# Two early output stores cut into pieces of unequal row counts, in an attention and mixture-of-adapters kernel

## The chip, the core and the metric

The kernel runs on one core of a Trainium2 chip. The metric is the device time of one execution in microseconds (us), as the median of several runs. The core has five engines that run side by side: TensorE (PE in the profile, its weight loads PEld), VectorE (DVE), ScalarE (ACT), GpSimd (POOL) and SyncE (SP). Memory is moved by 16 DMA engines that all queues share. A transfer that is issued by SP goes into SP's queue (q1), one issued by POOL into POOL's queue (q0). Each DMA engine adds one to a transfer's semaphore when its own part has landed, so that a transfer is complete at a count of 16.

## What is computed

Four batches of 6400 rows and 256 channels go through a cross-covariance attention, and the result goes through a mixture of eight low-rank adapters:

```
qn = q / (norm(q, axis=1) + 1e-06);  kn = k / (norm(k, axis=1) + 1e-06)
s = kn.transpose(0, 2, 1) @ qn / tau            # 256 x 256 per batch
a = softmax(s);  x = (v @ a).reshape(25600, 256)
logits = x @ w_gate                              # 8 experts, the best 2 are kept
w = softmax over the 2 kept logits
delta = sum over the 2 kept e of w[e] * ((x @ A[e]) @ B[e])
out = x + delta                                  # 25600 x 256, float32
```

All of q and k of a batch must have been read before its 256 x 256 matrix is known, and v is then multiplied by it. So 78 MB are read and 26 MB are written.

## The kernel before, in words

A batch's 6400 rows lie on 128 partitions, 50 rows of 256 channels on each. q and k are loaded in three parts of 17, 17 and 16 of these 50 (cast to bf16 on the way, L578), v in five parts of 10 (also L578). The output leaves in the same five parts per batch: the store of part i of batch b, written (b, i) here, takes 128 partitions of 10 x 256 float32, so each partition gives one run of 10,240 bytes, a **row** of the store in what follows. With 16 DMA engines each engine moves eight such rows per store. The last two parts of the last batch leave in three smaller stores each.

For each batch, PE accumulates k'q, k'k and q'q (`do_G`, L593 to L602), the norms and the softmax follow on DVE and ACT, and then every part of v is transposed (L788), gated (L812 to L879) and multiplied into the output tile `y` (`do_Y`, L915 and L920). ACT or DVE copy it from PSUM (`do_Ye`, helper lines L769 and L771), and the store follows (`do_store`, L928).

The order on each engine is written out ahead of time by a small planner (`make_plan` and `Plan.run`): it simulates the five engines and the DMA, and takes on each engine the step of lowest rank that is ready. Loads are issued by POOL in a fixed order, at most eight in flight, stores by SP. A planned store is one step on SP whatever its number of DMA instructions is, so the planner's order doesn't depend on how `do_store` issues it.

Some stores are held back on purpose. `HOLD` names for such a store a load, and `do_hold` (L645) puts a DMA of 32 bytes on SP's queue that reads the end of that load's tile. As SP issues in order, the stores behind it wait until that load has landed. SP's queue around the change is:

- 77.92 us: store (0, 2)
- 78.33 us: hold for k part 2 of batch 1
- 78.97 us: store (0, 1), and at 91.01 us store (0, 3)
- 166.65 us: hold for k part 1 of batch 3
- 167.21 us: store (0, 0), computed long before and held, and at 167.89 us store (1, 0)
- 182.74 us: hold for k part 2 of batch 3, and from 183.34 us on the rest of the stores

DMAs of SP and ACT take eight semaphores in turn; the DMA that gets a semaphore again waits for the one that had it before, eight places ahead.

Of the kernel before, what the change touches and what calls it, by code (L numbers as in the profile page):

```python
# [32 lines left out]
class Clock:  # L33


    WINDOW, FIRST, LOW, HIGH = 3.413, 0.31, 0.5, 0.8

# [3 lines left out]
    def at(self, t):  # L41
        w = max(0, int((t - self.FIRST) / self.WINDOW) + 1)
        while len(self.cold) <= w:
            share = self.busy[-1] / self.WINDOW
            self.cold.append(share < (self.HIGH if self.cold[-1] else self.LOW))
            self.busy.append(0.0)
        return w

    def took(self, t, us):

        end, w = t, self.at(t)
        while us > 1e-9:
            pace = 2.0 if self.cold[w] else 1.0
            step = min(us * pace, max(self.FIRST + w * self.WINDOW - end, 1e-6))
            self.busy[w] += step
# [5 lines left out]
    def idle(self, t):  # L61

        w = self.at(t)
        return t - self.FIRST - (w - 1) * self.WINDOW - self.busy[w] > self.SPARE

# [165 lines left out]
def make_plan(B, order, ahead):  # L231
# [150 lines left out]
    for b in range(B):  # L382
        for i in range(NP):
            x = pos["v", b, max(g for g, (i0, _) in enumerate(V) if i0 <= i)]
            parts = UNITS if b == B - 1 and i >= NP - FINE else ((0, PC),)
            for c, n in parts:
# [25 lines left out]

PARTS = {(0, 0): ((0, 2), (2, 15)), (0, 2): ((34, 8), (42, 8)), (3, 2): ((34, 8), (42, 8))}
FINE = 2
FIRST = 4
OFF = {(0, 0, 'k'), (0, 0, 'q'), (0, 1, 'q'), (0, 2, 'k'), (0, 2, 'q'), (0, 4, 'q'), (0, 5, 'q'),
        (0, 6, 'k'), (0, 6, 'q'), (0, 7, 'k'), (0, 8, 'q'), (1, 0, 'k'), (1, 0, 'q'), (1, 1, 'q'),
# [41 lines left out]
def kernel(  # L459
# [11 lines left out]
    nc = tc.nc  # L471

    B, N, C = q.shape
    P = 128
# [15 lines left out]
    out_v = out.rearrange("(b p c) d -> b p c d", b=B, p=P)  # L490
# [44 lines left out]
    held = {}  # L535
# [25 lines left out]
    def do_load(s, what, b, i, c, n):  # L561
        if what == "v":
            t, src, c0 = sb(s, "v", (b, i), [P, PC * max(n for _, n in V), C], BF16), v_v, c
        else:
            t = sb(s, "qk", (what, b, i), [P, max(n for _, n in QK), C], BF16)
            src, c0 = {"q": q_v, "k": k_v}[what], QK[i][0]
            if (b, c) == (0, 0):
                n = FIRST
                if "first" not in W:
# [6 lines left out]
        if (what, b, i) in (("q", 0, 0), ("k", 0, 0)):  # L576
            c, n = FIRST, c + n - FIRST
        nc.gpsimd.dma_start(t[:, c - c0:c - c0 + n, :], src[b, :, c:c + n, :])  # L578
# [346 lines left out]

    def do_store(s, b, i, c, n):
        lo = i * PC + c
        nc.sync.dma_start(out_v[b, :, lo:lo + n, :], held["y", (b, i), ""][:, c:c + n, :])  # L928


    do = dict(load=do_load, wts=do_wts, sq=do_sq, add=do_add, red=do_red, n2p=do_n2p, hold=do_hold, warm=do_warm, cast=do_cast, G=do_G, accs=do_accs, n2=do_n2, rsqrt=do_rsqrt, rq_ps=do_rq_ps, s=do_s,
              exp=do_exp, recip=do_recip, aT_ps=do_aT_ps, aT=do_aT, waA_ps=do_waA_ps, waA=do_waA,
              a=do_a, ZL=do_ZL, ZLe=do_ZLe, T=do_T, Te=do_Te, log=do_log, loge=do_loge, Z=do_Z, Ze=do_Ze, gzT=do_gzT,
              gzTe=do_gzTe, Y=do_Y, Ye=do_Ye, store=do_store)
    for name in ("m1", "eq1", "lm", "m2", "mask", "msum", "t", "th", "g2"):
        do[name] = gate_step(name)
# [50 lines left out]
```

## Time and profile before

| what | value |
|---|---|
| median of 4 runs | 254.39 us (254.31 to 254.58) |
| the profiled execution's own time | 254.36 us |
| its span from the first to the last instruction | 252.6 us |
| PE busy | 218.4 us (86% of the span) |
| DVE, ACT, POOL busy | 192.5, 151.5, 27.0 us |
| moved by DMA | 66.70 MB counted at the SBUF side, mean 264 GB/s |
| granted TensorE clock, mean | 0.980 |

A page of the profile has the busy time per engine, the span cut into 40 equal slices (a digit is the busy share in tenths, 9 is 90% or more), the DMA queues, the chain of work that ended last, the costliest groups of instructions, and the DMA issues with their median time from issue to landing. Other views of the same trace give the waits, the instructions in order of time, and tables by stretch of time. The trace also has, for each transfer, the times of the 16 counts on its semaphore and, for each DMA packet, its queue, start, duration and size; it doesn't have the number of the DMA engine that moved it.

### The profile page before, as it was taken

To read this page: it belongs to the slowest core of one execution; us is meant where nothing else is said; L and a number is where in the kernel's file an instruction comes from. 1 tells how busy PE (TensorE), PEld (TensorE's weight loads), DVE (VectorE), ACT (ScalarE), POOL (GpSimd) and SP (SyncE) were. 2 spreads that over 40 slices of the span, in tenths; PEclk is the share of its full clock that TensorE was granted. 3 is DMA by queue.
4 is the path that set the end of the run, shared out by engine and by line. 5 is a ranking of instruction groups with operands and counts; after the bars stand their busy time and mean duration, and the time that the engine had idled before them with its cause. 6 is when DMAs were issued, how large, how long until landed. Compare 5 with 4: busy or idle time off the path is not lost.

```text
span 252.6 us, 5852 instructions
## 1 busy us (share of the span) xinstructions
PE 218.4 (86%) x2357; PEld 194.1 (77%) x2357; DVE 192.5 (76%) x528; ACT 151.5 (60%) x269; POOL 27.0 (11%) x54
## 2 busy tenths in 40 slices
PE   0273997888999998899999999889999979999980
PEld 0151884676999997799899899779999768999970
DVE  0055587979988996988999987689898889888830
ACT  5354435555877545785677757452784846557770
POOL 7002110040002002000500100500000000000000
PEclk9998599999999999999999999999999999999997
DMA  8999999999999999999999999999999999999995
GB/s 251 213 219 209 214 219 214 214 219 215 215 215 223 308 305 294 246 215 221 210 214 218 220 214 218 215 208 324 309 254 335 337 317 319 342 400 428 419 410 227
DMA packets 11243, 66.70 MB, mean 264 GB/s; under 512 B 1360, under 2 KB 1744, under 8 KB 6608
## 3 DMA queue, kind: packets, MB, share of 16 engines
q0 software_dynamic: 6912, 38.80, 74.4%
q1 hardware_dynamic: 3968, 26.87, 26.1%
q10 hardware_dynamic: 336, 0.66, 0.8%
q8 instruction: 18, 0.29, 0.4%
q14 instruction: 9, 0.07, 0.1%
HBM read 78.91 MB, written 26.21 MB: 416 GB/s over the span
## 4 chain that ended last, share of the span: by engine, by line
PE 75%; DVE 10%; DMA 8%; ACT 2%; issue 2%; POOL 1%; DVEq 0%; POOLq 0%
PE Y_ps L915 17%; PE acc L593 16%; DMA qk<-in_k_dram 8%; PE Y_ps L920 8%; PE T_ps L788 7%; PE ZL_ps L812 6%; PE gzT_ps L902 5%; PE acc L597 5%; PE acc L602 4%; DVE a_bf L763 2%; PE Z_ps L879 1%; PE n2p_ps L636 1%; PE log_ps L826 1%; PE warm_ps L777 1%; DVE ssq L627 1%
## 5 line engine op out<-in xcount | busy, mean ns | idle before, releaser
L593 PE MATMUL acc<-qk 128*128 128x256 bf16 x400 | 70.3, 284 | 17.4 <-DMA qk<-in_k_dram 9.9
L915 PE MATMUL Y_ps<-a_bf,vT 128*128 128x256 bf16 x400 | 60.0, 272 | 0.2 <-DVE acc_sb L710 0.2
L621 DVE TENSOR_TENSOR ssq<-ssq,sq 128x1280 f32<-128x1280 f32 (+1 forms) x27 | 43.3, 1604 | 19.7 <-ACT sq L615 19.7
L769 ACT COPY y<-Y_ps 128x512 f32<-128x512 f32 x79 | 46.1, 585 | 17.0 <-PE Y_ps L920 13.9
L593 PEld LDWEIGHTS <-qk 128*128 128x128 bf16 x400 | 34.7, 102 | 20.6 <-DMA qk<-in_k_dram 10.8
L615 ACT ACTIVATE sq<-qk 128x1280 f32<-128x1280 bf16 (+1 forms) x27 | 36.9, 1367 | 18.9 <-DVE ssq L621 16.8
L915 PEld LDWEIGHTS <-vT 128*128 128x128 bf16 x400 | 39.0, 98 | 4.6 <-issue 0.3
L920 PE MATMUL Y_ps<-ball,gzT 128*128 128x256 bf16 x200 | 38.2, 273 | 0.0
L597 PE MATMUL acc<-qk 128*128 128x128 bf16 x242 | 34.9, 226 | 0.0
L769 ACT COPY vT<-T_ps 128x512 f32<-128x512 f32 (+1 forms) x44 | 21.2, 510 | 11.7 <-PE T_ps L788 11.3
L788 PE MATMUL T_ps<-ident,v 128*128 128x128 f32 x200 | 27.5, 274 | 0.6 <-DVE waA_sb L757 0.4
L597 PEld LDWEIGHTS <-qk 128*128 128x128 bf16 x242 | 24.7, 102 | 3.8
L890 DVE TENSOR_TENSOR gz<-zl,gateg 128x256 bf16<-128x256 f32 x70 | 26.3, 444 | 0.3
L578 POOL DMA_DIRECT2D v<-in_v_dram x20 | 11.4, 575 | 130.7 <-PE T_ps L788 88.6
L602 PE MATMUL acc<-qk 128*128 128x128 bf16 x168 | 23.9, 225 | 0.0
L788 PEld LDWEIGHTS T_ps<-ident,v 128*128 128x128 f32 x200 | 22.3, 141 | 1.6 <-DVE waA_sb L757 0.6
L902 PE MATMUL gzT_ps<-ident,gz 128*128 128x128 f32 x100 | 20.9, 281 | 2.6 <-DVE gateg L868 1.4
L920 PEld LDWEIGHTS <-gzT 128*128 128x128 bf16 x200 | 19.6, 98 | 2.3
L812 PE MATMUL ZL_ps<-waA_sb,vT 128*128 128x136 bf16 x280 | 19.5, 223 | 1.7 <-DVE waA_sb L757 1.5
L812 PEld LDWEIGHTS <-vT 128*128 128x128 bf16 x280 | 17.7, 98 | 2.4 <-issue 2.2
L771 DVE COPY gzT<-gzT_ps 128x256 f32<-128x256 f32 (+1 forms) x40 | 15.0, 379 | 4.7 <-PE gzT_ps L902 3.1
L771 DVE COPY y<-Y_ps 128x512 f32<-128x512 f32 x21 | 14.5, 700 | 4.1 <-PE Y_ps L920 4.1
(80 smaller groups left out, 268.9 us busy)
## 6 DMA issues: line engine op xcount, KB each, us to landing
out_dram<-y SPq DMA_DIRECT2D x18, 1280.0 KB, 17.5
v<-in_v_dram POOLq DMA_DIRECT2D x20, 640.0 KB, 19.0
qk<-in_q_dram POOLq DMA_DIRECT2D x7, 1088.0 KB, 21.4
qk<-in_k_dram POOLq DMA_DIRECT2D x7, 1088.0 KB, 27.4
qk<-in_q_dram POOLq DMA_DIRECT2D x4, 512.0 KB, 20.0
qk<-in_k_dram POOLq DMA_DIRECT2D x4, 512.0 KB, 23.2
qk<-in_q_dram POOLq DMA_DIRECT2D x2, 1024.0 KB, 19.2
qk<-in_k_dram POOLq DMA_DIRECT2D x2, 1024.0 KB, 23.5
```

What stands on the lines that cost most here:

```text
L593: nc.tensor.matmul(acc[ic][:, 0:256], kt[:, j, ic::CC], qt[:, j, :], start=c == 0, stop=False, skip_group_check=True)
L597: nc.tensor.matmul(acc[ic][:, 256:384], kt[:, j, ic::CC], kt[:, j, ic::CC], start=False, stop=False, skip_group_check=True)
L602: nc.tensor.matmul(acc[ic][:, 384:512], qt[:, j, ic * P:(ic + 1) * P], qt[:, j, ic * P:(ic + 1) * P], start=False, stop=c == NC - 1, skip_ ...
L615: nc.scalar.activation(out[:, 0:n, :], t[:, j:j + n, :], ACT.Square)
L621: nc.vector.tensor_tensor(out=t, in0=t, in1=held["sq", (w, b, g), ""][:, 0:n, :], op=OP.add)
L769: nc.scalar.copy(out, in_)
L771: nc.vector.tensor_copy(out, in_)
L788: nc.tensor.matmul(ps[:, j, :], vt[:, c + j, :].bitcast(FP32), W["ident32"], is_transpose=True, start=(j == 0), stop=(j == n - 1))
L812: nc.tensor.matmul(ps[:, j, :], vT_of(b, i, c + j)[:, :, ic], st[b]["waA"][:, ic, :], start=(j == 0 and ic == 0), stop=(j == n - 1 and ic ...
L902: nc.tensor.matmul(ps[:, j, :], pairs[:, j * P:(j + 1) * P], W["ident32"], is_transpose=True, start=(j == 0), stop=(j == n // 2 - 1))
L915: nc.tensor.matmul(ps[:, j, :], vT_of(b, i, c + j)[:, :, ic], st[b]["a"][:, ic, :], start=(j == 0 and ic == 0), stop=False, skip_group_che ...
L920: nc.tensor.matmul(ps[:, j, :], pair[:, :, j], W["B"], start=False, stop=(j == 1), skip_group_check=True)
```

## The change

Two stores are no longer issued as one DMA of 128 rows. Store (0, 2) is issued as three DMAs of 112, 8 and 8 rows, store (0, 0) as four DMAs of 96, 8, 13 and 11 rows. All other stores are as before, and the same bytes go to the same places. A DMA of 112 or 96 rows is dealt to 16 DMA engines, one of 8, 13 or 11 rows, as the change has it, to the first 8, 13 or 11 of them, one row each.

```diff
 FINE = 2
+SPLIT = {(0, 2): ((0, 112), (112, 8), (120, 8)), (0, 0): ((0, 96), (96, 8), (104, 13), (117, 11))}
 FIRST = 4
...
     def do_store(s, b, i, c, n):
         lo = i * PC + c
-        nc.sync.dma_start(out_v[b, :, lo:lo + n, :], held["y", (b, i), ""][:, c:c + n, :])
+        for p, rows in SPLIT.get((b, i), ((0, P),)):
+            nc.sync.dma_start(out_v[b, p:p + rows, lo:lo + n, :], held["y", (b, i), ""][p:p + rows, c:c + n, :])
```

The built program differs in these five added DMAs on SP and in which of the eight semaphores each later DMA of SP takes; the order of the instructions on every other engine is the same.

## The prediction

> **What bounds the kernel now.** I read the chain that ended last first, by line and then for its last 28 us. From 24.9 us on it runs on PE with short stretches of DVE and ACT; its only long DMA piece is the first k load. So between 25 and 246 us the loads are early enough. The end of the chain, followed by the SP queue in order of time:
>
> ```profile
> 244.94 0.44 PE Y_ps L915 x4
> 245.37 0.23 PE Y_ps L920 x2
> 245.63 0.58 ACT y L769
> ```
>
> ```profile
> 245.59 1.47 SPq L928 DMA_DIRECT2D out_dram<-y  x2
> ```
>
> The last product ends at 245.6 us, its copy at 246.2, and the last store is issued at 246.24. The span is 252.6. The remaining 6.4 us hold no computation, which the table by stretch of time shows (PE, PEld, DVE, ACT, POOL busy, clock, DMA share, GB/s):
>
> ```profile
> 246.00:248.00 2.00, 0.00 (x0) 0.00 (x0) 0.00 (x0) 0.21 (x1) 0.00 (x0) 1.00 1.01 400
> 248.00:250.00 2.00, 0.00 (x0) 0.00 (x0) 0.00 (x0) 0.00 (x0) 0.00 (x0) 0.81 0.73 294
> 250.00:252.60 2.60, 0.00 (x0) 0.00 (x0) 0.00 (x0) 0.00 (x0) 0.00 (x0) 0.50 0.14 54
> ```
>
> All 16 DMA engines work until 248 us, three quarters of their time is used until 250, and then 0.14: few engines are still at work while the others are done. The waits on SP's queue say that the end stands on these stores:
>
> ```profile
> SPq L982 <- DMA out_dram<-y: 4.3, 5, 1.2
> ```
>
> How far the engines lie apart is in the 16 counts on the semaphore of the last store (us, sorted):
>
> ```
> 248.74 248.81 248.82 248.92 249.00 249.28
> 250.09 250.51 250.52 250.53 250.70 250.83 250.94
> 251.58 251.74 251.83
> ```
>
> Six are early, seven in the middle, three late. The last count comes 0.72 us before the span ends, and nothing but that count is waited for. So the kernel ends with its latest DMA engine, and evening out the engines is worth at most 251.83 less the mean of the sixteen, 250.18, that is 1.65 us. Compute can't be overtaken: the early engines land 2.5 us after the issue, so they are bound by the issue at 246.24.
>
> **Does a shift at 80 or 170 us live to the end?** An engine's shift is lost only where that engine runs dry. The page's DMA row has 9 in all slices between the first and the last, and q0 and q1 together take 100.5% of 16 engines' time:
>
> ```profile
> DMA  8999999999999999999999999999999999999995
> ...
> q0 software_dynamic: 6912, 38.80, 74.4%
> q1 hardware_dynamic: 3968, 26.87, 26.1%
> ...
> q8 instruction: 18, 0.29, 0.4%
> ```
>
> The counts agree. Between the loads that land at 119 and at 149 us the sorted distances of the engines stay equal to about 0.1 us but for single steps, and the stores that land at 226, 230, 233, 236 and 240 us all have four early counts within 0.4 us and the last three 3.6 to 4.0 us behind the first. I take a shift as lasting, for the late engines at nothing lost; the early ones do run dry after about 240 us, as their distance shrinks to 3.1.
>
> **The change part by part.**
>
> - Price of a row: late full stores land 3.05 us apart on one engine (229.52, 232.58, 235.63 for the first count), eight rows each, 0.38 us a row; a row's packet lasts 385 ns alone and 398 beside a load. I take 0.385.
> - Rows per engine in the two stores, 8 + 8 = 16 before. After, as the change has them dealt: engines 0 to 7 get 7+1+1 and 6+1+1+1, 18 rows (+0.77 us); 8 to 10 get 7 and 8, 15 (-0.385); 11 and 12 get 14 (-0.77); 13 to 15 get 13 (-1.155).
> - Five more DMAs on SP, at 0.33 to 0.59 us of issue each by the rows of SP's queue. At 78 us two of them push the hold from 78.33 to about 79.3 and store (0, 1) from 78.97 to 79.9. Store (0, 2)'s rows start at 81.4 and land at 87.2 at the earliest, so q1 has work on each engine meanwhile: nothing. At 167 us three push store (1, 0) from 167.89 to about 169.4; the rows ahead of it land at 176.3 at the earliest: nothing. Without that cover it would be 1.5 us on q1 alone, while q0 kept the engines busy. The hold at 182.74 waits for its load and doesn't move.
> - Semaphores: later DMAs of SP wait for another DMA eight places ahead. The nearest new pair is the store issued at 185.9 us behind the 11-row piece, which lands near 178; each has 7 us or more. ACT and DVE copies that write the two `y` buffers again now wait for three and four semaphores in place of one; the waits view has no wait of ACT or DVE for a store at all, so it costs at most a few 20 ns semaphore instructions.
> - Small transfers: each adds a 4-byte packet (9 to 22 ns) per engine used, at most 0.1 us in all. Store after store in the end phase follows 6 ns behind the other's 4-byte packet on the same engine, so a transfer has no gap of its own while a queue is full. The Trainium skill, "DMA: Bandwidth & Descriptors", section "Anatomy of one DMA", speaks against the change: about 2.0 us fixed per DMA. Were that paid on the engines five times, the sum would be 264 us; the 6 ns row says that it is latency, and is hidden here.
>
> **Which engines are late** decides, and the trace has no engine numbers. What it tells: already in the first loads one engine trails (first big load: 15 counts within 0.67 us, the last at 1.16). Then 18 instruction blocks of 16 KB (q8) come, one every 10 us or so, 0.9 to 1.0 us each, and each sets one engine back by about 1.1. The first eight go to engines that were not late by a block from an earlier one, and the next ones to engines already late: at 164 us seven engines are still within 0.93, nine at 1.28 to 2.46. So the blocks go around about eight engines, 18 = 8 + 8 + 2, and the late three are those with a third block and the one that trailed from the start. An engine that trails by one block's worth before the first block is where I put the block before it; the late three are then neighbours in this round. I choose the numbering 15, 14, 13 for them: the last-served engine from the start is 15, and the round runs down. That is a choice, not a reading. Two other numberings stand below as rivals.
>
> On that choice the Trainium skill, same page, section "Latency and other measured facts", has a rule: engines 7 and 15 are usually slower than the rest. For 15 it fits; an engine 7 among the late three would give 255.1 us. No view here shows the numbers.
>
> **Sum.** The late three land at 251.83 - 1.155 = 250.67, and 8 to 12, from the middle, at 250.94 - 0.385 = 250.56 at the latest. But engines 0 to 7 are eight and only six are early, so two of the seven in the middle get 0.77 more. As the engines without blocks are the early ones, I take for them the two lowest of the middle, 250.09 and 250.51: 250.86 and 251.28. The last of these is then the new end, a gain of 251.83 - 251.28 = 0.55. The profiled execution took 254.36, the median is 254.39: **253.8 us**. The ends of this case are 253.2, where those two are so dry at the end that their shift is lost (only the late three count, 1.16 of gain), and 254.2, where a higher one of the middle is among them (250.94 + 0.77 = 251.71, 0.12 of gain).
>
> **Rivals.**
>
> 1. **A late engine has a number of 0 to 7.** It gets two rows more, 251.83 + 0.77: 255.1 us, slower. Any of the eight with a count over 251.06 is enough. For it: only three of sixteen are late, and by numbers alone they rarely all fall on 13 to 15. Against: seven engines get no block up to 164 us and the late three are neighbours, so all three lie among the engines with blocks.
> 2. **The round runs up**, late are 15, 8 and 9: the last two lose one row, 251.74 - 0.385 = 251.36, gain 0.47: 253.9.
> 3. **Rows of the 112- and 96-row DMAs cost more**, as engines take 7 or 6 neighbouring partitions in place of 8. No row shows it; below by nothing, above by the longest row or load packet of that stretch, 551 against 398 ns, 13 x 0.153 = 2.0 us on each engine: 251.83 - 1.155 + 2.0, 255.2 us. It decides from 89 ns a row.
> 4. **The pieces aren't dealt as said**: if an 8-, 8-, 8-, 13- and 11-row piece each went to one and the same engine, it would have 61 rows, 45 x 0.385 = 17 us more: some 265 to 271 us, less what later loads hide.
>
> **How the numbers follow.** The forecast's case 0.60 (0.44 of it faster by over 0.2%, which is 0.5 us and about what a measurement of this kernel can tell from no change; 0.16 within), rival 1 0.20 (slower), rival 2 0.10 (0.03 faster, 0.07 within), rival 3 0.07 and rival 4 0.03 (slower). Faster 0.47, same 0.23, slower 0.30. The range 253.2 to 255.2 takes in the forecast's own ends, rivals 1 and 2, and rival 3 up to its upper price.
>
> **What would show it.** Right: issue of the last store still at 246.2 us; its 16 counts span some 2.5 us instead of 3.1, the last near 251.3 and no group of three behind the rest; share of DMA after 250 us below 0.14. Wrong numbering: the last count at 252.5 or above with the first unchanged. Rival 3: the packets of the two split stores longer than 398 ns, and all 16 counts later. Wrong altogether: the last store issued at another time, or PE waiting for a load after 25 us.

## Result and profile after

The changed kernel takes 254.69 us (median of 41 runs, 254.38 to 255.61), the kernel before 254.48 us beside it (61 runs, 254.25 to 254.68). The ratio is 1.001, with a 95% interval of 1.0006 to 1.0015: slower by about 0.1%, which is within the 0.2% that the prediction took as no change. A gain of 0.55 us was forecast, and 0.2 us were lost. The ratios here and below compare fast runs with fast runs, and they can differ from the quotient of the two medians by 0.001, in the two slowest kernels by up to 0.002.

The profiled execution of the changed kernel took 254.86 us, 0.50 more than that of the kernel before and 0.17 above its own median, so it shows more than the typical loss. Its chain ends as before, one copy and a store, only later:

```profile
245.68 0.44 PE Y_ps L916 x4
246.12 0.23 PE Y_ps L921 x2
246.37 0.58 ACT y L770
```

SP's queue in order of time has the added DMAs in its counts (x3 and x5 where one and two stores stood), and, in a second window, the last two stores:

```profile
76.50 1.08 SPq L930 DMA_DIRECT2D out_dram<-y  x3
...
167.49 2.15 SPq L930 DMA_DIRECT2D out_dram<-y  x5
```

```profile
246.33 0.99 SPq L930 DMA_DIRECT2D out_dram<-y  x2
```

The last store is issued at 246.98 us (246.24 before). The table of the end by stretch of time, with the same columns as in the prediction:

```profile
246.00:248.00 2.00, 0.33 (x4) 0.05 (x1) 0.00 (x0) 0.89 (x2) 0.00 (x0) 1.00 1.05 420
248.00:250.00 2.00, 0.00 (x0) 0.00 (x0) 0.00 (x0) 0.00 (x0) 0.00 (x0) 0.60 0.85 337
250.00:253.10 3.10, 0.00 (x0) 0.00 (x0) 0.00 (x0) 0.00 (x0) 0.00 (x0) 0.50 0.12 46
```

The engines do lie closer together: more is moved from 248 to 250 us (337 GB/s, 294 before). But the stretch behind 250 us is 3.1 us long and not 2.6. The wait at the end and the load of the queues are as before:

```profile
SPq L984 <- DMA out_dram<-y: 4.6, 5, 1.2
```

```profile
DMA  8999999999999999999999999999999999999995
...
q0 software_dynamic: 6912, 38.80, 74.3%
q1 hardware_dynamic: 4016, 26.87, 26.1%
...
q8 instruction: 18, 0.29, 0.4%
```

q1 has 48 packets more, which are the small packets at the ends of the added DMAs; the bytes are the same. The mean row took 394.2 ns (393.4 before). The 16 counts on the last store's semaphore:

```
249.49 249.49 249.51 249.53 249.65 249.97 250.05 250.17
250.51 250.51 250.56 250.61 251.03 251.48 252.06 252.18
```

The group of three is gone, as forecast, but two engines stand 0.6 us behind the rest, and the last count is 0.35 us later than before. The counts span 2.69 us (3.09 before; some 2.5 were forecast). From the last count to the end of the span are 0.90 us, 0.72 before. So of the 0.53 us by which the span is longer, 0.35 lie ahead of the last count and 0.18 behind it. Both have to be explained.

### The profile page after: what moved, and what is told of

It reads as the page before. It is cut to its first block, busy times and chain, and to the rows that moved or that the text cites. A ratio compares the mean times of both kernels' runs of the same rounds, so it can differ in the third digit from the quotient of the medians.

```text
span 253.1 us, 5861 instructions
## 1 busy us (share of the span) xinstructions
PE 217.7 (86%) x2357; PEld 192.7 (76%) x2357; DVE 192.7 (76%) x528; ACT 151.2 (60%) x269; POOL 27.0 (11%) x54
## 4 chain that ended last, share of the span: by engine, by line
PE 45%; DMA 40%; issue 6%; DVE 3%; ACT 2%; POOL 1%; POOLq 0%; DVEq 0%
DMA v<-in_v_dram 17%; DMA qk<-in_k_dram 14%; PE Y_ps L916 12%; DMA qk<-in_q_dram 9%; PE acc L594 7%; PE Y_ps L921 6%; PE T_ps L789 5%; PE ZL_ps L813 4%; PE gzT_ps L903 4%; PE acc L598 2%; PE acc L603 1%; PE Z_ps L880 1%; POOL qk L579 1%; ACT a_exp L716 1%; PE log_ps L827 1%
## 5 line engine op out<-in xcount | busy, mean ns | idle before, releaser
L594 PEld LDWEIGHTS <-qk 128*128 128x128 bf16 x400 | 34.3, 101 | 21.5 <-DMA qk<-in_k_dram 12.4
L598 PE MATMUL acc<-qk 128*128 128x128 bf16 x242 | 34.4, 224 | 0.0
L598 PEld LDWEIGHTS <-qk 128*128 128x128 bf16 x242 | 24.2, 100 | 3.4
L603 PE MATMUL acc<-qk 128*128 128x128 bf16 x168 | 23.0, 218 | 0.0
L616 ACT ACTIVATE ssq<-qk 128x1536 f32<-128x1536 bf16 x8 | 11.9, 1488 | 11.5 <-DMA qk<-in_q_dram 7.1
```

Source lines behind the costliest of these rows:

```text
L594: nc.tensor.matmul(acc[ic][:, 0:256], kt[:, j, ic::CC], qt[:, j, :], start=c == 0, stop=False, skip_group_check=True)
L598: nc.tensor.matmul(acc[ic][:, 256:384], kt[:, j, ic::CC], kt[:, j, ic::CC], start=False, stop=False, skip_group_check=True)
L603: nc.tensor.matmul(acc[ic][:, 384:512], qt[:, j, ic * P:(ic + 1) * P], qt[:, j, ic * P:(ic + 1) * P], start=False, stop=c == NC - 1, skip_ ...
L616: nc.scalar.activation(out[:, 0:n, :], t[:, j:j + n, :], ACT.Square)
```

## Two readings

**First theory.** The view of the chain has changed: DMA has 40% of it (8% before), and loads that gate computation landed later. Load k part 2 of batch 3 has its last two counts at 182.2 and 183.5 us (182.7 and 182.7 before), PE waits for it, and computation, 0.2 us later than before up to there, is 0.7 us later from there on (the last store is issued at 246.98, before at 246.24). By this theory compute, late through one late engine, ends the kernel. **Rivals:** the added issues and pieces cost the time; or the end follows the latest engine alone, whatever compute does. The first group of kernels was to tell these apart.

## Experiments: one part, even pieces, another place

Each is the changed kernel with another table `SPLIT`; a piece is (first row, rows).

**Even pieces.**

```diff
+SPLIT = {(0, 2): ((0, 96), (96, 16), (112, 16)),
+         (0, 0): ((0, 64), (64, 32), (96, 16), (112, 16))}
```

> The same number of pieces (three for store (0, 2), four for store (0, 0)), but of 96, 16 and 16 and of 64, 32, 16 and 16 rows, so that every DMA engine keeps 16 rows in the two stores. The theory: three engines of 0 to 7 stood in the middle before, and two rows more make them the latest, so that the loads whose last count gates ACT or PE land later. Without a shift of rows all that is gone: the time of the kernel before, 254.4 to 254.6 us, the last store issued at 246.2 and the last count at 251.8. Rival one, five more DMA issues, semaphores or 4-byte packets cost the time: then it stays where the change is, 254.7, with the last store issued at about 247.0. Rival two, DMAs of fewer than 128 rows cost more per row: slower too, 254.7 or more, with packets of the two stores longer than 398 ns.

Measured: 254.57 us, the kernel before beside it 254.37; ratio 1.0009 (1.0001 to 1.0018). In its profiled execution the last store is issued at 246.50, the last count comes at 251.79 as in the kernel before (251.83), and the end 0.9 us behind it. So 0.1 to 0.2 us are lost without any shift of rows, and in the profiled execution all of it after the last count.

**Store (0, 2) alone.**

```diff
+SPLIT = {(0, 2): ((0, 112), (112, 8), (120, 8))}
```

> Only store (0, 2) is split (112, 8 and 8 rows), so engines 0 to 7 get one row more in all and 8 to 15 one less, from 87 us on. The theory: load q part 0 of batch 2 lands at about 100.5 us instead of 99.7, and ACT waits for it as with the whole change; load k part 2 of batch 3 lands later by 0.4 at most. Last store issued at 246.4 to 246.8, time 254.4 to 254.8. If store (0, 0) alone is what costs: 254.2 to 254.4, with the last store issued at 246.2 and about 0.2 gained at the end.

Measured: 254.48 us, ratio 1.0008 (0.9999 to 1.0017). Load q part 0 of batch 2 landed at 100.6 us, as the theory said, but it did so at 100.6 in the kernel with even pieces too. The last count comes at 251.60, 0.23 earlier than before, and yet nothing is gained: the end is 1.1 us behind it.

**Store (0, 0) alone.**

```diff
+SPLIT = {(0, 0): ((0, 96), (96, 8), (104, 13), (117, 11))}
```

> Only store (0, 0) is split (96, 8, 13 and 11 rows), from 167 us on: engines 0 to 7 get one row more, 11 and 12 one less, 13 to 15 two less. The theory: nothing changes up to 167 us (load q part 0 of batch 2 lands at 99.7 as before), load k part 2 of batch 3 lands at about 183.1 instead of 182.7, the last store is issued at 246.4 to 246.7, and the engines lie closer together at the end: 254.3 to 254.7. Rival, store (0, 2) alone is what costs: 254.2 or less, with the last store issued at 246.2 and the last count near 251.4.

Measured: 254.24 us, ratio 1.0003 (0.9994 to 1.0011). Last store issued at 246.43, last count at 251.42, which is 0.41 earlier than before. The theory had load q part 0 of batch 2 at 99.7 us as before, since nothing is changed ahead of 167 us; it landed at 100.4, so single loads move by 0.7 us without any cause in a split store. In these profiled executions each half of the change lowers the last count, and both together raise it, as one engine would do that has room for one row and not for two. But one program's last counts differ between executions too (252.18, 251.93 and 251.81 for the change, further below), so this only points that way.

**The same pieces later.**

```diff
+SPLIT = {(2, 2): ((0, 112), (112, 8), (120, 8)),
+         (2, 3): ((0, 96), (96, 8), (104, 13), (117, 11))}
```

> The same pieces, but cut out of the stores (2, 2) and (2, 3), which are issued at 200.8 and 212.8 us, after the last load of q and k. The theory: no load that gates ACT or PE is left behind them, so the last store is issued at 246.2 as before; the counts of the last store span 2.7 us instead of 3.1 as after the change, the last at about 251.5: 254.1 us, 0.3 to 0.4 below the kernel before. Rival, the five more issues or the pieces themselves cost the time: 254.7, with compute ending later. If the pieces that come late push single loads of v or the last stores' issues, 254.5 or more.

Measured: 257.31 us (six runs, 256.58 to 260.06), ratio 1.0135 (1.0098 to 1.0173): a miss for all theories. It was followed up with even pieces at the same place.

```diff
+SPLIT = {(2, 2): ((0, 96), (96, 16), (112, 16)),
+         (2, 3): ((0, 64), (64, 32), (96, 16), (112, 16))}
```

> The stores (2, 2) and (2, 3) in three and four pieces again, but even (96, 16, 16 and 64, 32, 16, 16 rows). The unequal pieces at this place gave 257.3, with SP's queue waiting for stores eight places ahead from 214 us on and one engine 1.6 us behind the next at the end. If that wait is what costs, since the pieces take five more of the eight semaphores while the queue is full: 256.5 us or more here too, and the last store issued after 247. If the uneven rows cost it: 254.4 to 254.9 us, with the counts of the last store within 3.2 us.

Measured: 260.52 us (six runs, 258.35 to 262.67), ratio 1.0224 (1.0192 to 1.0256), so uneven rows aren't the cause. SP's queue now waits for stores eight places ahead (three lines of waits, first the kernel with unequal, then the one with even pieces):

```profile
SPq L930 <- DMA out_dram<-y: 12.8, 4, 5.5
```

```profile
SPq L930 <- DMA out_dram<-y: 8.8, 3, 5.4
...
SPq L984 <- DMA out_dram<-y: 8.8, 5, 5.3
```

In the kernel before, no such line stands for its store line, L928. But there is more than a wait. In the tables by stretch of time (last two columns: DMA share, GB/s), even pieces first and the kernel before second, the engines are busy throughout and move less:

```profile
226.00:232.00 6.00, 6.00 (x82) 5.68 (x80) 5.64 (x21) 3.68 (x9) 0.00 (x0) 1.00 1.03 324
232.00:238.00 6.00, 6.00 (x70) 5.64 (x69) 4.98 (x16) 4.79 (x11) 0.00 (x0) 1.00 0.97 359
```

```profile
226.00:232.00 6.00, 6.00 (x75) 5.65 (x72) 5.41 (x21) 4.15 (x9) 0.00 (x0) 1.00 1.00 422
232.00:238.00 6.00, 6.00 (x76) 5.63 (x74) 5.21 (x17) 4.44 (x11) 0.00 (x0) 1.00 1.02 426
```

The rows of stores themselves were longer: from 226 to 232 us 515 ns on average (388 before), single ones up to 2.07 us. In the kernel with even pieces of the two early stores the rows around 85 and 175 us, beside loads, took 397 ns. What makes the later place slow (no loads beside the stores, the waits eight places ahead, or something else) was not separated and stays open.

**A larger dose, and its control.** Five early stores in pieces, once uneven and once even:

```diff
+SPLIT = dict.fromkeys(((0, 2), (0, 1), (0, 3), (0, 0), (1, 0)),
+                      ((0, 112), (112, 8), (120, 8)))
```

> A larger dose of the same shift: the five early stores (0, 2), (0, 1), (0, 3), (0, 0) and (1, 0) are each split into 112, 8 and 8 rows, so engines 0 to 7 get five rows more in all (1.9 us) and 8 to 15 five less. The theory, that engines of 0 to 7 become the latest and that the load which gates compute ends with the latest engine: load k part 2 of batch 3 lands 1 to 2 us later than in the same kernel with even pieces, the last store is issued 1 to 1.7 us later, the counts of the last store span 3.5 us or more; 256 to 257.5 us. Rival, the shift is harmless and the 0.1 to 0.3 us of the change are issues and pieces: as with even pieces, within 0.3 us.

```diff
+SPLIT = dict.fromkeys(((0, 2), (0, 1), (0, 3), (0, 0), (1, 0)),
+                      ((0, 96), (96, 16), (112, 16)))
```

> The control to the five splits: the same five stores in three pieces each, but of 96, 16 and 16 rows, so that every engine keeps its rows. The theory: ten more issues of SP are hidden, 254.4 to 254.6 us, last store issued at 246.2 to 246.6. Rival, issues, semaphores and 4-byte packets cost the time: twice the 0.2 us that five more issues with even pieces went with, 254.8 or more.

Measured: 256.40 us uneven, ratio 1.0075 (1.0062 to 1.0087), and 255.30 even, 1.0031 (1.0019 to 1.0043). The shift costs 1.1 us, as the theory has it, and ten more DMAs with even rows 0.8, as the rival has it. The chain of the uneven one shows the load that PE waits for (k part 2 of batch 3, issued at 161.21):

```profile
161.21 23.30 DMA qk<-in_k_dram
184.52 0.05 issue
184.56 0.39 PE acc L594 x2
```

Its last store is issued at 248.00 us, with even pieces at 245.87, so compute lies 2.1 us apart, and the times 1.1. The last counts lie 0.96 apart (253.12 and 252.16). The time follows the last count, not compute.

**Four engines instead of eight.**

```diff
+SPLIT = dict.fromkeys(((0, 2), (0, 0)), ((0, 112), (112, 4), (116, 4), (120, 4), (124, 4)))
```

> The shift goes to four engines in place of eight: the stores (0, 2) and (0, 0) are each split into 112 rows and four times 4, so engines 0 to 3 get six rows more in all (2.3 us) and 4 to 15 two less (0.77). If the three engines of 0 to 7 that stand in the middle or later are not among 0 to 3, four early engines fill up and all others come 0.77 earlier: load k part 2 of batch 3 lands at 182 us or before, the last count comes at 251.1 or before: 253.7 to 254.0 us. If one of them is among 0 to 3, it becomes the latest by far: load k part 2 of batch 3 1.5 to 2 us later, 255.8 to 257 us. Rival, only pieces and issues count, eight more of them: 254.6 to 254.8 either way.

Measured: 256.22 us, ratio 1.0070 (1.0057 to 1.0083). One engine is alone at the end: 254.24 us, the next 252.52. So one of the engines 0 to 3 already stood well back, and one was enough.

## Experiments: the engines by number

A piece of k rows goes to the first k engines, and its counts tell when these end. What the counts show is that a piece's engines are among those of every larger piece; the numbers follow the order in which rows are dealt, so "engine 3" is the fourth engine in that order. So the very last store of the **kernel before** was cut in several ways, and that of the changed kernel in one; the key in `do_store` gets the column as well:

```diff
+SPLIT = {(3, 4, 8): ((0, 112), (112, 9), (121, 5), (126, 2))}
...
+        for p, rows in SPLIT.get((b, i, c), ((0, P),)):
```

> A look that names DMA engines, made from the kernel before: only its very last store (2 x 256 elements a row) is cut into 112, 9, 5 and 2 rows, so that the counts of the pieces tell at which times the engines 0 to 8, 0 to 4 and 0 and 1 end. The theory: of the seven engines in the middle of the kernel before, three are among 0 to 7, and none of the late three is. So among the counts of the 9-row piece three or four lie 1.2 us or more behind the first, and none in the last group. Rival one, a late engine has a number of 0 to 7: a count of these pieces in the last group, within 0.5 us of the latest. Rival two, 0 to 7 are all early and the shift of rows is not what costs: all counts of the 5- and the 2-row piece within 0.6 us of the earliest. Time 254.4 to 255.5 us, of no meaning.

> The same with pieces of 112, 7, 6 and 3 rows: the counts name the engines 0 to 6, 0 to 5 and 0 to 2. Expected as for the look before: of the engines 0 to 6 two or three lie in the middle, 1.2 us or more behind the first, none in the last group. Rivals as there.

> The same with pieces of 112, 11, 4 and 1 rows: the counts name the engines 0 to 10, 0 to 3 and engine 0. By the theory and the kernel with six more rows on engines 0 to 3, which took 256.2 us, at least one of 0 to 3 lies in the middle, 1.2 us or more behind the first, and with 8 to 10 one early engine and two of the middle are added. Rival: 0 to 3 all early, then the time of that kernel has another cause.

> The same with pieces of 96, 13, 11 and 8 rows, which names the groups of the change: 0 to 7, 8 to 10, 11 and 12, 13 to 15. The theory: the late three are 11 or 12 and two of 13 to 15, the third of 13 to 15 is early, 8 to 10 has one early engine, 0 to 7 has five early or nearly so and three in the middle. The choice of the prediction, all three of 13 to 15 late, would show as three counts that only the 96-row piece has in the last group.

> A look at engine 3 by itself in the kernel before: the very last store in pieces of 112, 9, 4 and 3 rows, whose counts name the engines 0 to 8, 0 to 3 and 0 to 2; the count that the 4-row piece has and the 3-row piece lacks is engine 3's. The theory: engine 3 ends 1.1 to 1.5 us behind the first engine, 0.7 to 0.9 before the two latest. Rival: engine 3 is early, and another of 0 to 2 stands there. Time 254.2 to 254.6, of no meaning.

> The same look at the changed kernel (two early stores split as in the change, the very last store in pieces of 112, 9, 4 and 3 rows). The theory: engine 3, with two rows more, is now the latest of all, 251.6 to 252.2 us, and the two that were latest have come down to about 251.0 to 251.4. Rival: the latest is not engine 3 but one of 4 to 15.

How such counts are read, with the 9, 4 and 3 rows in the kernel before (us; a piece of k rows has k + 1 counts, of which the first, under 1 us after the issue, belongs to no row):

```
112 rows: 249.47 249.53 249.63 249.79 249.79 250.10 250.28 250.28
          250.38 250.88 250.97 250.98 250.99 251.10 251.72 251.82
9 rows:   248.05 | 249.64 249.83 249.96 249.97 250.27 250.47 250.48 250.57 251.18
4 rows:   248.86 | 250.14 250.15 250.45 251.36
3 rows:   249.18 | 250.32 250.32 250.62
```

Each engine's count is 0.17 to 0.19 us later than its count of the piece before. The 3-row piece continues 250.14, 250.15 and 250.45; so engine 3 is the 251.36 of the 4-row piece, 251.18 of the 9-row piece and 250.99 of the first. The other three cuts give the same: engine 3 at 250.97, 251.08 and 251.00 by elimination, engines 0 and 1 within 0.35 us of the first. With pieces of 96, 13, 11 and 8 rows the two latest, 251.79 and 251.82, have no successor in the 13-row piece, whose last count is 251.22: both have numbers of 13 to 15. Engines 0 to 7 are there three early ones, four from 250.32 to 250.46, and one, by the above engine 3, near 250.85. The third engine of 13 to 15 is early: the 13-row piece has all nine counts of the middle and four of the five early ones.

The changed kernel in the same way:

```
112 rows: 249.26 249.41 249.49 249.56 249.73 249.90 249.96 250.31
          250.37 250.71 250.81 250.83 250.88 251.33 251.43 251.93
9 rows:   247.91 | 249.43 249.65 249.77 249.91 250.48 251.06 251.52 251.63 252.10
4 rows:   248.73 | 249.63 250.09 250.66 252.28
3 rows:   249.04 | 249.81 250.26 250.83
```

Engine 3 is the latest of all, at 251.93 (252.28 less two steps), 0.94 us later than in the kernel before. The next two, 251.43 and 251.33, go on in the 9-row piece and so have numbers below 9. The two of 13 to 15 that were at 251.72 and 251.82 are thus at 250.88 or less.

These kernels settle the first theory too. Their times, one run each, were 254.24 to 254.59 us, and the kernel before next to them had 254.33 and 254.51. In one of them (96, 13, 11 and 8 rows; 254.33 us) the chain ends at

```profile
246.42 0.23 PE Y_ps L921 x2
246.65 0.02 issue
246.67 0.58 ACT y L770
```

and the first piece of the last store is issued at 247.28, 1.04 us later than in the profiled execution of the kernel before; its last count comes at 251.82 and its span is 252.6 us as there. Up to that store the programs are the same. So compute may end a microsecond later and the kernel doesn't, and **the first theory falls**: what counts ahead of the last count is the latest engine.

## What lies behind the last count

SP waits at the very end for its eight DMA semaphores, one instruction after the other and always in the same order. In the trace of the kernel before, and then of the changed one (start, end, the two semaphores that an instruction waits for; us):

```
251.21 251.23 SP EVENT_SEMAPHORE $S[117] $S[113]
251.84 251.87 SP EVENT_SEMAPHORE $S[118] $S[114]
251.91 251.92 SP DRAIN
```

```
252.19 252.22 SP EVENT_SEMAPHORE $S[111] $S[100]
252.25 252.28 SP EVENT_SEMAPHORE $S[116] $S[99]
252.31 252.34 SP EVENT_SEMAPHORE $S[117] $S[113]
252.37 252.40 SP EVENT_SEMAPHORE $S[118] $S[114]
252.44 252.45 SP DRAIN
```

The last store's semaphore was the last of the eight (118). DMAs take the eight in turn, so five more move it to 111, and three more waits of 0.06 us, 0.18 in all, stand behind the last count. The time of a profiled execution less its last count is a clock for this:

| kernel | added DMAs | waits behind the last store's | own time less last count, us |
|---|---|---|---|
| before; 4-row pieces on engines 0 to 3 | 0; 8 | 0 | 2.53; 2.54 |
| changed; even pieces | 5; 5 | 3 | 2.68; 2.69 |
| store (0, 0) alone | 3 | 5 | 2.81 |
| store (0, 2) alone | 2 | 6 | 2.88 |

This is where the two half changes lost what their last counts had gained. The two kernels with ten added DMAs have six waits too but 3.14 us. The other 0.26 lies outside the span: their spans end 1.09 us behind the last count, as with store (0, 2) alone (1.10), but their own time less the span is 2.05 us, against 1.77 to 1.81 in all other traces. Why is not known.

## Experiments: each cause on its own

All four ran on one chip, with the kernel before at 254.38 us.

**Eight added DMAs in place of five**, the change with one more store in four even pieces:

```diff
 SPLIT = {(0, 2): ((0, 112), (112, 8), (120, 8)), (0, 0): ((0, 96), (96, 8), (104, 13), (117, 11)),
+         (0, 1): ((0, 64), (64, 32), (96, 16), (112, 16))}
```

> The change with three more even pieces (store (0, 1) as 64, 32, 16 and 16 rows), so that eight DMAs are added in place of five and the last store gets the same semaphore as in the kernel before. At the end SP waits for eight semaphores one after the other, 0.06 us each; after the change the last store's is the fifth, so three more waits stand behind its last count, 0.19 us. Theory: the end comes 0.75 to 0.8 us after the last count instead of 0.92, which is 0.19 less than the change in the same call, less up to 0.1 for three more pieces: 254.5 to 254.6 us. Rival, every added piece costs 0.04 us or more on each engine and the order of the semaphores nothing: 254.8 or more.

> The change itself once more, beside the others on the same chip: 254.6 to 254.75 us; last count 252.0 to 252.2, 0.9 us before the end of the span.

Measured: 254.55 us, ratio 1.0002 (0.9987 to 1.0016), and the change itself 254.74, 1.0015 (1.0005 to 1.0024). The difference of 0.19 is as expected, but the intervals overlap, so the times alone don't prove it. The own time less the last count does: 2.51 and 2.71 us. The change's last counts were 251.38 and then one engine alone at 251.81; with 252.18 and 251.93 in its other two traces the latest engine ends between 251.8 and 252.2. With eight added DMAs it was alone too, and later: 252.33, the next 251.66.

**Without engine 3, and with it.** The first has 13 and 3 rows, the second 12 and 4 in their place, with all else as here:

```diff
+SPLIT = {(0, 2): ((0, 112), (112, 13), (125, 3)), (0, 0): ((0, 112), (112, 13), (125, 3)),
+         (0, 1): ((0, 64), (64, 32), (96, 16), (112, 16)), (0, 3): ((0, 112), (112, 16))}
```

> Stores (0, 2) and (0, 0) as 112, 13 and 3 rows each: engines 0 to 2 get two rows more, 3 to 12 keep 16, 13 to 15 lose two (0.77 us). Four even pieces more in stores (0, 1) and (0, 3) bring the added DMAs to eight, so that the last store has its old semaphore. By the named engines 0 to 2 are early (lags of 0 to 0.5 us) and the two latest are among 13 to 15, so the last count falls from 251.8 to about 251.1, where engine 3 and one of 11 and 12 stand: 253.6 to 253.9 us, 0.5 to 0.8 below the kernel before. Rival, compute sets the end, not the latest engine: 254.3 to 254.5. Rival, pieces cost what they save: 254.3 or more.

> As the kernel beside it, but 112, 12 and 4 rows twice, so that engine 3 gets two rows more as well and engine 12 loses two. Nothing else differs. Theory: engine 3 stands at 250.97 to 251.08 before and comes to 251.75 to 251.85, so that the last count is back where it was: 254.3 to 254.6 us, 0.6 to 0.8 more than with 13 and 3 rows. Rival, engine 3 isn't what stops the change (any eight engines with two rows more would): within 0.2 us of the kernel with 13 and 3 rows.

Measured: 254.01 us with 13 and 3 rows, ratio 0.9987 (0.9978 to 0.9996), and 254.53 with 12 and 4, 1.0015 (1.0005 to 1.0025). One row more or less on engine 3 in each of two stores (and the reverse on engine 12, which is not among the latest) is worth 0.5 us, and decides the sign. The counts of the last store with 13 and 3 rows, then with 12 and 4:

```
249.17 249.19 249.22 249.29 249.31 250.33 250.34 250.75
250.83 251.03 251.05 251.15 251.26 251.26 251.33 251.50
```

```
249.05 249.05 249.16 249.32 249.56 250.02 250.29 250.45
250.59 250.76 251.14 251.15 251.15 251.21 251.43 252.17
```

With 13 and 3 rows no engine stands apart any more; with 12 and 4 one does. The version with 13 and 3 rows beats both kernels, if by little. It gave 0.4 us where 0.5 to 0.8 were expected, since the last count came to 251.50 and not 251.1. Its end by stretch of time:

```profile
246.00:248.00 2.00, 0.00 (x0) 0.00 (x0) 0.00 (x0) 0.59 (x1) 0.00 (x0) 1.00 1.03 414
248.00:250.00 2.00, 0.00 (x0) 0.00 (x0) 0.00 (x0) 0.00 (x0) 0.00 (x0) 0.88 0.82 330
250.00:252.20 2.20, 0.00 (x0) 0.00 (x0) 0.00 (x0) 0.00 (x0) 0.00 (x0) 0.50 0.20 76
```

As much is moved from 248 to 250 us as after the change (330 and 337 GB/s), but the last stretch is 2.2 us long, not 3.1.

## Why the prediction was wrong, step by step

- **The kernel ends with its latest DMA engine: right**, with the waits behind its last count. In every trace the own time is the last count plus 2.5 to 2.9 us (3.1 in two), whether the last store was issued at 245.9 or at 248.0.
- **A shift lasts to the end, at 0.385 us a row: right in kind.** Engine 3 got two rows more and ended 0.94 us later, where 0.77 was reckoned.
- **The late engines are 15, 14 and 13: right for the two that count.** Both latest are among 13 to 15, and in the changed kernel they came down to 250.88 or less. That is luck in part, as the numbering was a choice. The third of that group is early. The reading of three late engines was too wide as well: of the stores listed for it, the first three have only two counts 3.6 us or more behind the first and the third at 2.8, and the five kernels in which only the last store is cut have two late counts, not three. Rival 1 falls in its own form, no late engine has a number of 0 to 7, but its addition, any of the eight over 251.06, was nearly met by engine 3 (250.97 to 251.08), and slower is what it had forecast. Rival 2 falls, as both latest are among 13 to 15.
- **"I take for them the two lowest of the middle group": this step failed.** Five of the engines 0 to 7 stood in the middle, not two, and one of them, engine 3, was at its upper end (250.99), one row's reach from the late ones. 250.99 + 0.77 is 251.76, which is the prediction's own case of "a higher one of the middle" (251.71, 0.12 of gain). That case was given as the end of a range and was the likelier one: with five of eight in the middle it is a poor bet that the highest is not among them. The reason that was given, that engines without instruction blocks are the early ones and have the low numbers, does not hold: only three of the eight are early.
- **Semaphores: the sum lacked a term.** It counted waits of later DMAs and of copies, and found none, rightly. It left out that the last store changes its place among the eight waits at the end: 0.18 us, nearly all of the 0.2 us by which the medians differ.
- **Small transfers, "at most 0.1 us in all": too low, and no fixed price.** The latest engine, reckoned from 250.99 and its added rows, ended 0.05 to 0.42 us beyond that in the three traces of the change, 0.4 and 0.6 beyond it with eight added DMAs (12 and 4 rows, and the change with one more store cut), 0.9 in the kernel with 4-row pieces, and 0.2 with ten. With even rows five added DMAs moved the last count by nothing and ten by 0.33. As executions with the same early stores scatter by 0.35 us too (251.72 to 252.07 where only the last store is cut), what these parts of a microsecond come from stays open.
- The sum with these sizes, from the two traces that name engine 3: 250.99 + 0.77 + 0.17 = 251.93, where 0.17 is what was measured beyond the two rows in that trace. That is 0.1 later than the 251.83 of before, and with 0.18 behind it 0.3 in all. Measured: 0.2 us in the first comparison, 0.36 in the last. So the shift gained nothing, and the wait at the end made it a loss.
- **Five issues on SP hidden: right.** With even pieces the last count stayed at 251.79. **Rival 3**, longer rows in the pieces, falls: the rows of the two split stores (the 1st to 128th and the 385th to 512th on SP's queue, in order of their start) took 398.2 and 398.0 ns on average, 397.9 and 396.9 before, where 89 ns more would have decided. **Rival 4** falls with the counts: a piece of 9 rows ends on nine engines.
- **"Wrong altogether: the last store issued at another time"** came true (246.98) and was a bad test. Programs that are the same up to the last store put it at 246.24 in one execution and 247.28 in another, with the same time.
- The Trainium skill, "DMA: Bandwidth & Descriptors", section "Anatomy of one DMA", gives about 2.0 us fixed per DMA, for DMAs that GpSimd issues, and puts most of it down to the wait until the last byte has landed. Here, on SP's queue, ten added DMAs with even rows moved the last count by 0.33 us; by an estimate from the section's figure it would have been some 20, had the engines paid it each time. The prediction's reading, that it is latency and hidden, holds.

## What to carry to other kernels

Where a kernel ends with its latest DMA engine, find out which engine that is before rows are moved: a last store cut into pieces for the first 9, 4 and 3 engines names them. What a shift gives to some it takes from others, so the bound is the latest of those that receive, not the mean of their group. And count what stands behind the last transfer: here the number of DMAs, taken modulo eight, was worth up to 0.35 us between the last count and the end.

## What had not been expected

- The end of compute moves by a microsecond between executions of programs that are the same up to the last store, and the time by 0.1 us; what the chain that ended last is made of moves with it (PE 75% and 45%, DMA 8% and 40% in the two kernels), so it was a poor guide to what sets the end.
- A DMA of k rows (1 to 13 here) has k + 1 counts: one 0.4 to 1.0 us after its issue, and one for each engine that moves a row.
- Cutting the stores (2, 2) and (2, 3), issued at 200.8 and 212.8 us in the kernel before, cost 3 to 6 us, where the same pieces of two early stores cost about 0.2 us. With even pieces, rows took 515 ns on average and up to 2.07 us from 226 to 232 us. The cause is open.
